# Moving a transform's last product behind another small product, its copies, and a dozen load times, in a fused FFT and mixture-of-experts kernel

## The chip, the cores and the metric

The kernel runs on one core of a Trainium2 chip. The metric is the device time of one execution, in microseconds (us), as the median of several runs. The core has a matrix engine (TensorE, PE in the profile; PEld is its weight load), a vector engine (VectorE, DVE), a scalar engine (ScalarE, ACT), a general engine (GpSimd, POOL) and a queue that issues nearly all transfers (SyncE, SP). Each runs its own instructions strictly in order.

## The reference

Everything is in 32-bit floats. A filter in the frequency domain runs along the sequence of each of 8 batches; its output, 24576 rows of 256, goes through a squared-ReLU layer and then through a soft mixture of experts whose slots are filled by a softmax over *all* rows:

```python
X = np.fft.rfft(x, axis=1)                       # x: 8 x 3072 x 256
y = np.fft.irfft(X * (filt_r + 1j * filt_i), n=3072, axis=1)
x = y.reshape(24576, 256)
h = np.maximum(x @ w_in, 0.0)                    # 256 -> 2048
x = h * h @ w_out                                # 2048 -> 256
logits = x @ phi                                 # 32 slots
d = softmax of logits over the rows;   slot_input = d.T @ x
slot_out[e] = np.maximum(slot_input[e] @ w1[e], 0.0) @ w2[e]   # 8 experts, 4 slots each
c = softmax of logits over the slots;  out = c @ slot_out
```

## The kernel before

The rows are cut into 48 chunks of 512, six per batch. A chunk is eight **pairs**; a pair makes two blocks of 128 of the hidden layer, each from six matmuls of 128x512 (lines 594 to 596: the data are split into a leading part `xo[:, 0]` and a remainder `xo[:, 1]`, the weights likewise). ACT takes each block out of PSUM with a ReLU (L601); the first block is squared on ACT (L603), the second on POOL (L605); DVE transposes both (L622). `xo` has two buffers, so a chunk's data are written while the chunk before runs.

The order of everything else is written out by hand. Time is counted in **units**: pair P stands at 2P, a chunk is 16 units, and within a pair there are four steps of half a unit, each with three of the six matmuls of a block. Work is put into five streams (`dsp`, `mv`, `late`, `fft`, `w`), each an event list with a unit as its due time; `run_streams` hands out what is due before and after each step, and holds back what needs PSUM banks until enough of the five side banks are free. "Unit 9.5 of a chunk" below is the due time modulo 16.

What is put there, and matters here:

- **Logits** (`logit`, L663): two groups of 16 matmuls in a chunk, at units 1.5 and 9.5, on a 128x32 division of the array.
- **Slots product** (`slot_in`, L793, `dispatch_events`): 32 matmuls on the same division, at unit 9.5 of the chunk that follows, right behind the logits. It reads `hd`, a rearranged copy of the hidden data that 16 transfers per chunk make (`move`, L651), and `eT`. For chunk 0 it is `slot_blocks` (L810), then `keep_block` and `sum_blocks`.
- **Inverse over n1** (`out_events`): the last product of the transform. `mm_y` (L514, 64 matmuls on a 64x64 division) reads `gin`, loaded by `load_g`; `even_y` (ACT) and two `unfold` (DVE, L531) undo a folding; `lead_y` (ACT, L539) writes the leading part of `xo` and `rest_y` (POOL, L546) its remainder, each once for either half `k` of the 256 columns. So 45 of the 48 chunks; three take another path.
- **Forward transform of the next batch** (`fft_events`): `load_x`, `fold_x` (an add on DVE, L155, and a subtraction on POOL, L156, for either `k`), `mm_a` (L165), stores to memory, then four rounds of `mm_b` (L299), filter `filt` (DVE, L310) and `join` (POOL, L319), and `mm_g2` (L218), with loads `load_f2` (filter, 1 MB), `load_s2`, `load_w` and `load_v`. Its wide tiles share three buffers.
- **The end**: the last chunk's softmax, the experts (`layer1`, `layer2`) and the output product. The experts' weights are loaded by `load_experts` into 6 tiles `w1t` (22 transfers of 256 KB), and into others.

Of the kernel before, what the change touches and what calls it, by code (L numbers as in the profile page):

```python
# [6 lines left out]
F32 = mybir.dt.float32  # L7
# [3 lines left out]
ALU = mybir.AluOpType  # L11
# [27 lines left out]
def body(tc, x, cA, cAf, fwp, fwd, ivp, inv, flt, cst, w_in, w_out, phi, w1, w2, out):  # L39
# [414 lines left out]
    def out_events(b, st, late):  # L454
# [92 lines left out]

        for g in range(NCB):
            if 6 * b + g not in (0, 1, 6):
                T = 96 * b + 16 * g - 12  # L550
                late(max(T - 14, 13.5), load_g, g)
                late(T, mm_y, g)
                late(T + 0.5, even_y, g)
                late(T + 1, unfold, g, ALU.add)
                late(T + 1.5, unfold, g, ALU.subtract)
                for k in range(2):
                    late(T + 5.5 + 2 * k, lead_y, g, k)
                    late(T + 6.5 + 2 * k, rest_y, g, k)
                continue
            T = 96 * b + 16 * g - 4  # L560
            put = late
            if T < 0:
                def put(t, fn, *a):
                    put0(ST["G0"] + ST["Gd"] * (t + 7), fn, *a)
            put(T - (5 if (b, g) == (0, 1) else 3), load_g, g)
            if T < 0:
                put(T - 1, warm)
            for k in range(2):
                put(T + k, mm_ai, g, k)
                put(T + k + 0.5, lead_ai, g, k)  # L570
                put(T + k + 0.5, rest_ai, g, k)
# [121 lines left out]


    run = {}

    def dispatch_events(c, put):
        q = 16 * (c + 1) + (2 if c else 6)
# [183 lines left out]
        if c == NCH - 1:  # L882
# [1 line left out]
                evac_l, gather, emax, expo, rescale, turn_e, turn_l, slot_blocks, keep_block, sum_block,  # L884
                row_max, row_exp, row_out, store_c,
            )
        put(q + .5, evac_l)
        put(q + 1.5, gather)
        put(q + 2.5, emax)
        put(q + 4, expo)  # L890
        put(q + 4, turn_l)
        put(q + 5, rescale)
        put(q + 5.5, turn_e)
        if c == 0:
            put(q + 7.5, slot_blocks)
            for r in range(4):
                put(q + 9 + .5 * r, keep_block, r)
            put(q + 11.5, sum_blocks)
        else:
            put(q + 7.5, slot_in)  # L900
            put(q + 9, accum)
# [199 lines left out]
    with tc.manual_schedule():  # L1101
        put, late = stream("fft"), stream("late")
# [14 lines left out]
        for j in range(4):  # L1117
# [3 lines left out]
            w = 1024 // len(ops)  # L1121
# [5 lines left out]
        for n in range(4):  # L1127
# [2 lines left out]
                wput(WO[n][1][k], conv_wo, n, k)  # L1130

        LEAD = [
            [[5.5] * 4, [3.5] * 4, [5] * 4, [5.5] * 4],
            [[5.5, 7.5, 15.25, 15.25], [6.5, 12.5, 13.5, 13.5], [5, 5.5, 10, 10], [5.5, 13, 15.25, 15.25]],
            [[20.25] + [15.25] * 3, [13.5] * 4, [20.5, 10, 10, 10], [8, 15.25, 15.25, 15.25]],
        ]

        opened = False
# [6 lines left out]
        for b in range(1, NB):  # L1145
            st = {}
            if b == 1:
                when = ([(22, 25, 28), (24, 29, 33.5), (27.5, 32, 36.5)], [47, 54.5, 65.5, 76.5], [53, 61.5, 70.5, 81.5])
            elif b == 2:
                when = ([(-19, -15.5, -10), (-11, -7, -3), (-5.5, -3, 0)], [13.5, 22, 38, 54], [18.5, 33.5, 49.5, 65.5])  # L1150
            else:
                when = ([(-35, -31, -26), (-23, -19, -14.5), (-22.5, -15.5, -10)], [1.5, 22, 38, 54], [17.5, 33.5, 49.5, 65.5])
            fft_events(b, lambda: G["fft"], stream("fft", 96 * (b - 1)), *when, dict(f=3, u=8, c=2, lead=LEAD[min(b, 3) - 1]), st)
            out_events(b, st, late)
        for c in range(NCH - 1):
            dispatch_events(c, stream("dsp"))
            if c:
                for n in range(4):
                    t = 0.5 * (n // 2)
                    for q, p in enumerate((14, 15, 16, 18) if c == 1 else (10, 11, 14, 18)):  # L1160
                        stream("mv", 16 * c)(p + t, move, c, q, n)
        for f in range(2, 8, 2):
            stream("mv", 16 * (NCH - 1))(5.5 + f / 2, late_turns, 2)
# [50 lines left out]
        w1t = []  # L1214
        for P in range(NP + 2):
            if P == 11:
                open_fft()
            if P == 48 * (NB - 1):
                G["fft_c"].__exit__(None, None, None)
                G["w1_c"], w1p = pool("w1p")  # L1220
                for n in range(6):
                    m = 4 if n < 5 else 2
                    w1t.append(w1p.tile([128, m * 512], F32, tag=f"w{n}", name="w1t"))
                    load_experts(w1t[-1], m, 0)
            if P == NP - 7:
                early = G["mlp"].tile([128, 8 * D], F32, tag="xo", name="wx", bufs=2)
                load_experts(early, 0, 3)
# [52 lines left out]
        w = (NB * N2 - 8) // 4  # L1280
# [6 lines left out]
        def load_call(n):  # L1287
            o = w * (n % 2)
            sync.dma_start(out=c_all[n // 2][:, o:o + w], in_=c_dr[:, 8 + w * n:8 + w * n + w])
# [6 lines left out]
        for r in range(4):  # L1296
            p = st["S"][r]
# [10 lines left out]
        load_experts(dsp.tile([128, 512], F32, tag="et", name="wx"), 0, 2)  # L1308
        load_experts(dsp.tile([128, 2 * 512], F32, tag="ac", name="wx"), 0, 3)
        row_max()  # L1310
        row_exp()
        row_out()
        store_c()
        load_call(3)
        p = bank("s0")
        for j in range(16):
            c4 = j % 4
# [6 lines left out]
        p = bank("s1")  # L1324
        for k in range(2):
            pe.matmul(p[:, 32 * k:32 * k + 32], af[:, 128 * k:128 * k + 128], s32, start=True, stop=True)
        si = dsp.tile([128, 2, NS], F32, name="si")
        vec.tensor_copy(si, p[:, 0:64].rearrange("p (k s) -> p k s", s=NS))
        vec.memset(zt, 0.0)

        hs.append([dsp.tile([128, 512], F32, tag="eT", name="hs", bufs=2) for h in range(2)])
# [51 lines left out]
        p = bank("s4")  # L1383
# [12 lines left out]
        for g in range(NG):  # L1396
            b, o = divmod(g, N2 // 4)
# [3 lines left out]
            for h in range(2):  # L1401
                p = bank(("s0", "s1", "s2", "s3")[ops % 4]).rearrange("p (a d) -> p a d", d=D)
# [166 lines left out]
```

## Time and profile before

| | |
|---|---|
| runs, us | 1882.72, 1887.92, 1883.05 (median 1883.05) |
| the profiled execution, us | 1880.15 |
| its span, us | 1878.2 |
| mean granted clock of TensorE | 0.994 |
| PE busy | 1824.0 us (97%) |
| DVE, ACT, POOL busy | 1206.0 (64%), 1034.8 (55%), 774.4 (41%) |
| matmuls of L594, L595, L596 | 626.6, 605.1 and 605.8 us |
| L663, L793, L514 (matmuls) | 186.3, 169.0, 53.2 us |

"Busy" is the share of the span in which an engine had an instruction running. Matmuls overlap: a 128x512 matmul is drawn 0.39 to 0.40 us long, while the next starts 0.23 us after it, so a gap of less than about 0.16 us between two doesn't show as idle time. The clock is the share of full speed that the chip granted TensorE: 1 is 2.4 GHz, and its other level is 1.2 GHz.

### The profile page before, as it was taken

Reading aid. Unit: us, or ns where it says so; the run is one execution under the profiler, and the core shown is the slowest. Engines: PE = TensorE matmul, PEld = TensorE weight load, DVE = VectorE, ACT = ScalarE, POOL = GpSimd, SP = SyncE. Lnnn points to the kernel's source line nnn. Section 1 sums busy time; section 2 is a strip of 40 time slices with the busy share of each in tenths; the row PEclk is TensorE's granted clock in tenths of the full one; section 3 lists DMA queues with packets and bytes.
Section 4 is the critical chain, followed back from the end, with each engine's and each line's share of the span. In section 5 each row is a group of like instructions: output and inputs, shape, how many; then the busy total and the mean of one; then the engine's idle time right before and its main releaser. Section 6 shows DMA issues by size and latency. Waiting matters only on the chain.

```text
span 1878.2 us, 42103 instructions
## 1 busy us (share of the span) xinstructions
PE 1824.0 (97%) x16326; PEld 1196.4 (64%) x16326; DVE 1206.0 (64%) x2267; ACT 1034.8 (55%) x1930; POOL 774.4 (41%) x812
## 2 busy tenths in 40 slices
PE   9999999999999999999999999999999999999987
PEld 6656566666666666666666666666666665666555
DVE  7946655766667666666567666666566755565558
ACT  6754455555555555555555555555555555455445
POOL 4043443534444544434444544444444533333224
PEclk9999999999999999999999999999999999999999
DMA  9768788886977697786978698787977677564989
GB/s 310 217 177 253 216 236 246 234 246 195 266 209 215 194 263 220 213 242 176 280 210 224 179 264 238 192 234 194 273 218 227 179 193 221 150 178 115 247 327 382
DMA packets 245813, 425.02 MB, mean 226 GB/s; under 512 B 25712, under 2 KB 103664, under 8 KB 245616
## 3 DMA queue, kind: packets, MB, share of 16 engines
q1 hardware_dynamic: 244744, 421.13, 77.6%
q8 instruction: 130, 2.13, 0.5%
q10 hardware_dynamic: 728, 1.15, 0.2%
q14 instruction: 67, 0.55, 0.1%
q0 software_dynamic: 144, 0.07, 0.0%
HBM read 151.71 MB, written 77.59 MB: 122 GB/s over the span
## 4 chain that ended last, share of the span: by engine, by line
PE 84%; DMA 6%; DVE 3%; SPq 3%; issue 2%; ACT 1%; POOL 0%; DVEq 0%; ACTq 0%
PE p L594 18%; PE p L596 17%; PE p L595 17%; PE sd L793 9%; PE L L663 8%; PE sd L299 3%; PE sd L514 2%; PE sd L218 2%; PE sd L165 2%; SPq L651 2%; DMA f<-x 2%; DMA hd<-hT 1%; DMA f<-flt 1%; DVE ct L1204 1%; PE pt L1193 1%
## 5 line engine op out<-in xcount | busy, mean ns | idle before, releaser
L601 ACT ACTIVATE h<-p 128x512 f32<-128x512 f32 x768 | 459.2, 598 | 545.8 <-PE p L596 527.9
L605 POOL TENSOR_TENSOR h<-h 128x512 f32<-128x512 f32 x375 | 393.7, 1050 | 816.6 <-ACT h L601 733.5
L622 DVE STREAM_TRANSPOSE hT<-h 128x512 f32<-128x512 f32 x736 | 490.2, 694 | 350.0 <-ACT h L603 295.4
L594 PE MATMUL p<-xo,wiH 128*128 128x512 f32 x1534 | 626.6, 408 | 0.0
L596 PE MATMUL p<-xo,wiL 128*128 128x512 f32 x1534 | 605.8, 395 | 0.0
L595 PE MATMUL p<-xo,wiH 128*128 128x512 f32 x1534 | 605.1, 394 | 0.0
L594 PEld LDWEIGHTS p<-xo,wiH 128*128 128x128 f32 x1534 | 288.5, 188 | 156.5 <-issue 81.8
L596 PEld LDWEIGHTS p<-xo,wiL 128*128 128x128 f32 x1534 | 288.7, 188 | 68.5
L595 PEld LDWEIGHTS p<-xo,wiH 128*128 128x128 f32 x1534 | 289.2, 188 | 58.7
L603 ACT ACTIVATE h<-h 128x512 f32<-128x512 f32 x393 | 249.0, 633 | 12.5
L319 POOL TENSOR_TENSOR u<-u 128x256 f32<-128x256 f32 x224 | 161.1, 742 | 131.1 <-DVE u L310 131.0
L663 PE MATMUL L<-h,wf 128*32 128x512 f32 x1536 | 186.3, 598 | 2.2 <-DVE wf L1017 1.8
L793 PE MATMUL sd<-hd,eT 128*32 128x512 f32 x1472 | 169.0, 597 | 6.9 <-DMA hd<-hT 6.9
L310 DVE TENSOR_TENSOR u<-sd,f 128x512 f32<-128x512 f32 x240 | 153.0, 676 | 16.4 <-DMA f<-flt 9.2
L793 PEld LDWEIGHTS sd<-hd,eT 128*32 128x32 f32 x1472 | 48.2, 111 | 119.3 <-issue 105.8
L546 POOL TENSOR_TENSOR xo<-gin,xo 128x512 fp32r<-128x512 f32 x90 | 119.1, 1324 | 0.0
L228 ACT ACTIVATE f<-sd 128x512 f32<-128x512 f32 x112 | 61.0, 608 | 87.3 <-PE sd L218 87.3
L854 DVE SCALAR_TENSOR_TENSOR ac<-ac,sc,sd 128x512 f32<-128x512 f32 x46 | 34.4, 748 | 105.9 <-PE sd L793 105.9
L663 PEld LDWEIGHTS L<-h,wf 128*32 128x32 f32 x1536 | 40.4, 109 | 95.2 <-issue 89.7
L712 DVE TENSOR_TENSOR lo<-L,lp 128x512 fp32r<-128x512 f32 x47 | 32.2, 685 | 73.3 <-ACT lp L711 73.2
L156 POOL TENSOR_TENSOR f<-f 128x512 f32<-128x512 f32 x42 | 54.1, 1288 | 57.0 <-DVE u L155 38.0
L769 DVE STREAM_TRANSPOSE eT<-et 32x128 f32<-32x128 f32 x184 | 72.3, 393 | 1.9
(161 smaller groups left out, 1596.8 us busy)
## 6 DMA issues: line engine op xcount, KB each, us to landing
hd<-hT SPq DMA_DIRECT2D x736, 256.0 KB
f<-flt SPq DMA_DIRECT2D x28, 1024.0 KB
gin<-G SPq DMA_DIRECT2D x47, 512.0 KB
out<-w1t SPq DMA_DIRECT2D x47, 512.0 KB
f<-x SPq DMA_DIRECT2D x84, 256.0 KB
S<-f SPq DMA_DIRECT2D x42, 512.0 KB
f<-S SPq DMA_DIRECT2D x112, 192.0 KB
G<-f SPq DMA_DIRECT2D x112, 192.0 KB
```

Source lines behind the costliest of these rows:

```text
L310: vec.tensor_tensor(out=u, in0=p.rearrange("p (h d) -> p h d", d=D), in1=f[:, 2 * r + k:2 * r + k + 1, :].to_broadcast([128, 2, D]), op=AL ...
L319: gps.tensor_tensor(out=a[:, h, :], in0=a[:, h, :], in1=b[:, 1 - h, :], op=ALU.add if h else ALU.subtract)
L546: gps.tensor_tensor(out=lo, in0=st["gi", g][:, k::2, :], in1=hi, op=ALU.subtract)
L594: pe.matmul(p, wh, x[:, 0, kk, :], start=(kk == 0), stop=False)
L595: pe.matmul(p, wh, x[:, 1, kk, :], start=False, stop=False)
L596: pe.matmul(p, wl, x[:, 0, kk, :], start=False, stop=(kk == 1))
L601: act.activation(out=h, in_=p, func=ACTF.Relu, scale=2.0 ** -8)
L603: act.activation(out=h, in_=h, func=ACTF.Square)
L605: gps.tensor_tensor(out=h, in0=h, in1=h, op=ALU.mult)
L622: vec.transpose(hT[c, f // 8][:, f // 4 % 2, :, o:o + 128], h2[P, k].rearrange("p (b t) -> p b t", b=4))
L663: pe.matmul(lg[c][32 * n:32 * n + 32, :], wf[:, f, :], h2.pop((P + n // 2, n % 2)), start=(f < 4), stop=(f >= FT - 4), tile_position=(0, 3 ...
L793: pe.matmul(S[32 * n:32 * n + 32, :], e[:, 32 * t:32 * t + 32], v, start=(t == 0), stop=(t == 3), tile_position=(0, 32 * n),)
```

## The change

Six things, all of them in the order; no arithmetic is added or removed.

1. `mm_y` moves from unit 4 to unit 9.5 of the chunk before its own, where it stands right behind `slot_in`. With it move `even_y` (4.5 to 10), both `unfold` (5 and 5.5 to 10.5), `lead_y` (9.5 and 11.5 to 11.5 and 13.5) and `rest_y` (10.5 and 12.5 to 12 and 14). `load_g` stays where it was.
2. Chunk 0's own steps (`evac_l` to `sum_blocks`) come 0.5 to 2 units earlier (list `FIRST`), and the transfers `move` of chunk 1 1.5 units earlier in three of four parts; the first fold and `mm_a` of batch 1 come 0.5 and 1.5 units earlier.
3. Batch 1's loads (`LEAD[0]`, in the order `load_w`, `load_v`, `load_f2`, `load_s2`, four rounds each) come up to 6.5 units earlier.
4. From batch 3 on, the first `load_x` comes 6 units earlier, and the first `load_s2` 2 units later.
5. The 22 transfers of `w1t` are spread over six places, unit 6 of chunks 42 to 46 and unit 12 of chunk 46, instead of all at once at the start of chunk 42.
6. At the end, the last chunk's `row_exp`, `row_out`, `store_c` and `load_call(3)` stand behind the product that gives `si` instead of ahead of it.

```diff
-                T = 96 * b + 16 * g - 12
-                late(max(T - 14, 13.5), load_g, g)
+                T = 96 * b + 16 * g - 6.5
+                late(max(T - 19.5, 13.5), load_g, g)
                 late(T, mm_y, g)
                 late(T + 0.5, even_y, g)
                 late(T + 1, unfold, g, ALU.add)
-                late(T + 1.5, unfold, g, ALU.subtract)
+                late(T + 1, unfold, g, ALU.subtract)
                 for k in range(2):
-                    late(T + 5.5 + 2 * k, lead_y, g, k)
-                    late(T + 6.5 + 2 * k, rest_y, g, k)
+                    late(T + 2 + 2 * k, lead_y, g, k)
+                    late(T + 2.5 + 2 * k, rest_y, g, k)
...
+    FIRST = [22, 23, 24, 25, 25, 26, 28]
...
         if c == 0:
-            put(q + 7.5, slot_blocks)
+            for t, fn in zip(FIRST, (evac_l, gather, emax, expo, turn_l, turn_e, slot_blocks)):
+                put(t, fn)
...
-            [[5.5] * 4, [3.5] * 4, [5] * 4, [5.5] * 4],
+            [[6.5, 6.5, 9.5, 9.5], [10, 7.5, 8, 10], [5, 6, 6.5, 6.5], [5.5, 10.5, 10, 10]],
...
-                when = ([(22, 25, 28), (24, 29, 33.5), (27.5, 32, 36.5)], ...
+                when = ([(22, 24.5, 26.5), (24, 29, 33.5), (27.5, 32, 36.5)], ...
...
-                when = ([(-35, -31, -26), (-23, -19, -14.5), (-22.5, -15.5, -10)], ...
+                when = ([(-41, -31, -26), (-23, -19, -14.5), (-22.5, -15.5, -10)], ...
...
-                    for q, p in enumerate((14, 15, 16, 18) if c == 1 else (10, 11, 14, 18)):
+                    for q, p in enumerate((12.5, 13.5, 14.5, 18) if c == 1 else (10, 11, 14, 18)):
...
-                for n in range(6):
-                    m = 4 if n < 5 else 2
-                    w1t.append(w1p.tile([128, m * 512], F32, tag=f"w{n}", name="w1t"))
-                    load_experts(w1t[-1], m, 0)
+            if P in (339, 347, 355, 363, 371, 374):
+                n = len(w1t)
+                m = 4 if n < 5 else 2
+                w1t.append(w1p.tile([128, m * 512], F32, tag=f"w{n}", name="w1t"))
+                load_experts(w1t[-1], m, 0)
...
         row_max()
-        row_exp()
-        row_out()
-        store_c()
-        load_call(3)
...
         vec.tensor_copy(si, p[:, 0:64].rearrange("p (k s) -> p k s", s=NS))
+        row_exp()
+        row_out()
+        store_c()
+        load_call(3)
```

On PE, in a chunk near the middle of the program, before: the inverse's group (L514) stands alone between two steps of three matmuls, behind the two matmuls of `gather` (L722, L723).

```order
L722 MATMUL sd<-lp,ss_t 128x512
L723 MATMUL sd<-lo,ss_t 128x512
L594 MATMUL p<-xo,wiH 128x512
L595 MATMUL p<-xo,wiH 128x512
L596 MATMUL p<-xo,wiL 128x512
L514 MATMUL sd<-cst_t,gin 64x2x32 x32
```

And now, in the same chunk, behind the logits (L663) and the slots product (L794 in the changed file, L793 before):

```order
L594 MATMUL p<-xo,wiH 128x512
L595 MATMUL p<-xo,wiH 128x512
L596 MATMUL p<-xo,wiL 128x512
L663 MATMUL L<-h,wf 32x512 x8
L794 MATMUL sd<-hd,eT 32x512 x16
L514 MATMUL sd<-cst_t,gin 64x2x32 x32
```

Three small products stand in one row where there were a row of two and one alone; this is so in 44 chunks (one x here is two matmuls of the trace).

On POOL, in the chunk of a batch in which the second third of the next batch is folded, before: `xo` is the remainder (`rest_y`), `f_...` a fold, `h` a square.

```order
L546 TENSOR_TENSOR xo<-gin,xo 128x512
L605 TENSOR_TENSOR h<-h 128x512
L546 TENSOR_TENSOR xo<-gin,xo 128x512
L156 TENSOR_TENSOR f_15373<-f_15373 128x512
L605 TENSOR_TENSOR h<-h 128x512
L156 TENSOR_TENSOR f_15373<-f_15373 128x512
```

And now:

```order
L605 TENSOR_TENSOR h<-h 128x512 x5
L546 TENSOR_TENSOR xo<-gin,xo 128x512
L156 TENSOR_TENSOR f_15336<-f_15336 128x512
L605 TENSOR_TENSOR h<-h 128x512
L546 TENSOR_TENSOR xo<-gin,xo 128x512
L156 TENSOR_TENSOR f_15336<-f_15336 128x512
```

The second remainder stood ahead of the fold; now a fold and one more square stand ahead of it. In the other chunks only the square does.

On SP, at the start of chunk 42, before: `hd` is a move, `w1t` the experts' weights.

```order
L460 DMA gin<-G 128x1024
L651 DMA hd<-hT 128x1x512 x12
L1085 DMA w1t<-w 128x512 x22
L651 DMA hd<-hT 128x1x512 x4
L880 DMA c_dr<-co 128x128
```

And now, from the same move on:

```order
L651 DMA hd<-hT 128x1x512 x16
L881 DMA c_dr<-co 128x128
L1089 DMA w1t<-w 128x512 x4
L460 DMA gin<-G 128x1024
L651 DMA hd<-hT 128x1x512 x16
```

The last four moves of a chunk no longer stand behind 22 weight transfers; four of these stand ahead of each of the next loads of `gin`.

## Rows read from the trace of the kernel before

**Rows 1.** Busy time by stretch: length, engines' busy us (count), clock, DMA share, GB/s.

```profile
110.00:305.00 195.00, 183.13 (x1688) 114.89 (x1684) 113.48 (x213) 97.83 (x184) 85.19 (x88) 0.98 0.80 222
305.00:1575.00 1270.00, 1265.44 (x11456) 826.29 (x11452) 819.92 (x1555) 708.24 (x1311) 566.77 (x583) 1.00 0.79 221
1595.00:1604.00 9.00, 5.29 (x27) 1.25 (x28) 1.31 (x3) 0.00 (x0) 0.00 (x0) 0.62 0.50 164
```

**Rows 2.** Timeline of PE: start, length, line, matmul, count; small products joined and alone.

```profile
1156.22 0.40 PE L596 MATMUL p<-xo,wiL 128*128 128x512 f32 x1
1156.55 1.92 PE L663 MATMUL L<-h,wf 128*32 128x512 f32 x16
1158.40 1.96 PE L299 MATMUL sd<-f,fw 48*32 48x256 f32 x64
...
1160.63 0.39 PE L595 MATMUL p<-xo,wiH 128*128 128x512 f32 x1
...
1197.96 1.16 PE L514 MATMUL sd<-cst_t,gin 64*64 64x64 f32 x64
...
1201.71 0.40 PE L596 MATMUL p<-xo,wiL 128*128 128x512 f32 x1
1202.04 1.96 PE L299 MATMUL sd<-f,fw 48*32 48x256 f32 x64
...
1204.26 0.39 PE L595 MATMUL p<-xo,wiH 128*128 128x512 f32 x1
...
1646.49 0.40 PE L596 MATMUL p<-xo,wiL 128*128 128x512 f32 x1
1646.82 1.92 PE L663 MATMUL L<-h,wf 128*32 128x512 f32 x16
...
1649.01 0.39 PE L595 MATMUL p<-xo,wiH 128*128 128x512 f32 x1
```

**Rows 3.** Timeline of PE: chunk 32's slots product and the first matmul of chunk 33.

```profile
1246.36 3.62 PE L793 MATMUL sd<-hd,eT 128*32 128x512 f32 x32
...
1258.40 0.40 PE L594 MATMUL p<-xo,wiH 128*128 128x512 f32 x1
```

**Rows 4.** Timeline of POOL in the same stretch: idle time and its releaser in brackets.

```profile
1253.95 1.04 POOL L605 TENSOR_TENSOR h<-h 128x512 f32<-128x512 f32 x1 [1.52 <-ACT h L601]
1254.95 1.35 POOL L546 TENSOR_TENSOR xo<-gin,xo 128x512 fp32r<-128x512 f32 x1
1256.48 1.04 POOL L605 TENSOR_TENSOR h<-h 128x512 f32<-128x512 f32 x1 [0.18 <-ACT h L601]
```

**Rows 5.** Timeline of POOL: the fold ahead of the start of chunk 35.

```profile
1328.81 1.30 POOL L156 TENSOR_TENSOR f<-f 128x512 f32<-128x512 f32 x1 [0.63 <-DVE u L155]
1330.07 1.49 POOL L605 TENSOR_TENSOR h<-h 128x512 f32<-128x512 f32 x1
```

**Rows 6.** Timeline of DVE, five places.

```profile
138.41 1.31 DVE L622 STREAM_TRANSPOSE hT<-h 128x512 f32<-128x512 f32 x2 [7.03 <-DMA hd<-hT]
...
223.07 1.29 DVE L310 TENSOR_TENSOR u<-sd,f 128x512 f32<-128x512 f32 x2 [6.64 <-DMA f<-flt]
...
875.00 0.69 DVE L155 TENSOR_TENSOR u<-f 128x512 f32<-128x512 f32 x1 [5.48 <-DMA f<-x]
...
1326.95 1.79 DVE L155 TENSOR_TENSOR u<-f 128x512 f32<-128x512 f32 x1
...
1787.32 0.48 DVE L1323 TENSOR_SCALAR af<-pt,fz 128x256 f32<-128x256 f32 x1
```

**Rows 7.** Timeline of SP: the issue of the experts' weights.

```profile
1575.53 15.46 SPq L1085 DMA_DIRECT2D w1t<-w  x22
```

**Rows 8.** Timeline of PE: a wait in chunk 5, and one in chunk 42.

```profile
262.94 3.48 PE L218 MATMUL sd<-u,iv 32*64 32x256 f32 x64 [3.07 <-DMA iv<-inv]
...
1590.79 1.03 PE L793 MATMUL sd<-hd,eT 128*32 128x512 f32 x6
1598.71 5.24 PE L793 MATMUL sd<-hd,eT 128*32 128x512 f32 x26 [6.88 <-DMA hd<-hT]
```

More of the change, by code (lines that the diff above doesn't have):

```diff
@@ L886, in dispatch_events @@
             )
[L887 to L893, printed above, removed]
-        if c == 0:
-            put(q + 7.5, slot_blocks)
+        if c == 0:
+            for t, fn in zip(FIRST, (evac_l, gather, emax, expo, turn_l, turn_e, slot_blocks)):
+                put(t, fn)
+        else:
+            put(q + .5, evac_l)
+            put(q + 1.5, gather)
+            put(q + 2.5, emax)
+            put(q + 4, expo)
+            put(q + 4, turn_l)
+            put(q + 5, rescale)
+            put(q + 5.5, turn_e)
+        if c == 0:
             for r in range(4):
-                put(q + 9 + .5 * r, keep_block, r)
-            put(q + 11.5, sum_blocks)
+                put(FIRST[-1] + 1 + .5 * r, keep_block, r)
+            put(FIRST[-1] + 3.5, sum_blocks)
         else:
@@ L1132, in body @@
         LEAD = [
-            [[5.5] * 4, [3.5] * 4, [5] * 4, [5.5] * 4],
+            [[6.5, 6.5, 9.5, 9.5], [10, 7.5, 8, 10], [5, 6, 6.5, 6.5], [5.5, 10.5, 10, 10]],
             [[5.5, 7.5, 15.25, 15.25], [6.5, 12.5, 13.5, 13.5], [5, 5.5, 10, 10], [5.5, 13, 15.25, 15.25]],
-            [[20.25] + [15.25] * 3, [13.5] * 4, [20.5, 10, 10, 10], [8, 15.25, 15.25, 15.25]],
+            [[20.25] + [15.25] * 3, [13.5] * 4, [20.5, 10, 10, 10], [6, 15.25, 15.25, 15.25]],
         ]
@@ L1147, in body @@
             if b == 1:
-                when = ([(22, 25, 28), (24, 29, 33.5), (27.5, 32, 36.5)], [47, 54.5, 65.5, 76.5], [53, 61.5, 70.5, 81.5])
+                when = ([(22, 24.5, 26.5), (24, 29, 33.5), (27.5, 32, 36.5)], [47, 54.5, 65.5, 76.5], [53, 61.5, 70.5, 81.5])
             elif b == 2:
@@ L1151, in body @@
             else:
-                when = ([(-35, -31, -26), (-23, -19, -14.5), (-22.5, -15.5, -10)], [1.5, 22, 38, 54], [17.5, 33.5, 49.5, 65.5])
+                when = ([(-41, -31, -26), (-23, -19, -14.5), (-22.5, -15.5, -10)], [1.5, 22, 38, 54], [17.5, 33.5, 49.5, 65.5])
             fft_events(b, lambda: G["fft"], stream("fft", 96 * (b - 1)), *when, dict(f=3, u=8, c=2, lead=LEAD[min(b, 3) - 1]), st)
```

## The prediction, made before the changed kernel ran

> **What bounds the kernel now.** The first view to read is busy time by stretch [rows 1]. From 305 to 1575 us, two thirds of the span, PE idles 1270 − 1265.44 = 4.6 us in all, at full clock, while DVE, ACT and POOL have a third to a little over a half of their time free. So the other engines and the transfers count only where PE waits for them; elsewhere the time is the number of matmuls and what lies between them. In the opening, 110 to 305, PE idles 195 − 183.13 = 11.9 us and the clock falls to 0.98 of full speed, which costs about another 195 × 0.02 = 3.9 (at the lower of the two levels everything takes twice as long). A third place is a hole of some 13 us near 1595. The reader should look for three things: what stands between matmuls, the few holes, and who will deliver PE's data last once work is moved.
>
> **The joined product.** PE's timeline [rows 2] gives the price of changing the way the array is divided. From the last full matmul (L596) ahead of a small product to the second full one (L595) behind it: the logits alone take 1649.01 − 1646.49 = 2.52 us, the L299 product alone 1204.26 − 1201.71 = 2.55, both in a row 1160.63 − 1156.22 = 4.41. Each span holds two full matmuls; 36 of them fill the stretch from the end of the slots product, 1246.36 + 3.62 = 1249.98, to the next chunk at 1258.40 [rows 3], so one takes 8.42 / 36 = 0.234 and two 0.47. Joining saves 2.52 + 2.55 − 0.47 − 4.41 = 0.19 us. The change does the same with L514, alone before [rows 2], in 44 chunks. Its 64x64 division behind a 128x32 one isn't in the trace; the nearest is this pair, also of two divisions. 44 × 0.19 = **8.4 us off**; from zero (the change of division inside the row costs as much as leaving it) to twice that.
>
> **Its copies.** This step can give it back. Before, the second remainder was written well ahead of the chunk's start. In chunk 32 take E = 1249.98, the end of the slots product, and S = 1258.40, the next chunk's first matmul [rows 3]; S = E + 8.4. POOL's last remainder ended at 1254.95 + 1.35 = 1256.30 [rows 4], 2.1 us before S. Now it is due 1.5 units later, behind the next square. That square began at 1256.48, with no copy ahead of its ReLU on ACT; the square before it, which had one (`lead_y` due at unit 11.5), began at 1253.95 [rows 4], and a pair is 12 × 0.234 = 2.8 us, so with a copy ahead it begins near 1256.75, ends near 1257.8, and the remainder ends near 1259.15, S + 0.75. PE needs it for its fifth matmul, at S + 4 × 0.234 = S + 0.94, whose weights are loaded one matmul ahead, at S + 0.7. So in an ordinary chunk it arrives just as it is wanted: 0 to 0.1 us late. 38 chunks: I take 0.5 us, bounds 0 and 4. The moved product itself hides nothing and needs nothing: E is 1.1 us later with S later by the same.
>
> In five chunks (11, 17, 23, 29, 35) a fold now stands ahead as well. Before chunk 35 the fold on POOL ran from 1328.81 to 1330.11, as DVE's add (1326.95, 1.79 long) let it go, and the square behind it from 1330.07 for 1.49 [rows 5, 6]. The remainder would follow at 1331.56 and end at 1332.9; that chunk's first matmul was at 1330.2 by the same 8.4 us, so it is wanted at 1330.9. That is 2.0 us late, 1.55 if the square takes 1.04 as in [rows 4]. I take 1.8: 5 × 1.8 = **9 us on**. Nothing hides it: PE has only that chunk's matmuls to do. It could be nothing, if POOL ran ahead, so the bounds are 0 and 12. In chunks 2 and 5 other work stands there; 1.5 us on for both.
>
> Why DVE's add took 1.79 us in one place and 0.69 in another [rows 6] bears on this: the long one began just as POOL ran a remainder. The Trainium skill's page "SBUF — State Buffer" (SBUF: two separate sides) says that a DVE operation with two SBUF inputs and a GpSimd operation exclude each other for a whole instruction. By that rule the next add of the fold could also get in ahead of the late remainder, and the nine would be about 12; the trace agrees with the rule where the two met.
>
> **The weights of the experts.** On SP, 22 transfers take 15.46 us to issue [rows 7] and stand between the moves of one chunk. The slots product that needs the last four stops after 6 of its matmuls, waits 6.88 us, and does the other 26 in 5.24 us instead of some 2.9, at a granted clock of 0.62 [rows 1, 8]: from 1590.79 to 1603.95 it takes 13.2 us where 3.62 is usual [rows 3]. Spread in fours, each group costs SP 4 × 15.46 / 22 = 2.8 us of issue, at unit 6, four units ahead of the moves. Behind them in SP's queue stands only a load of `gin` wanted some 19 units later. So the whole difference goes: **9.5 us off**, 7 if some moves are pushed.
>
> **The loads of x.** Once per batch from batch 3 on, DVE stood at the fold's first add until x arrived, 5.48 us in the worst case [rows 6], and everything behind it on DVE with it. There are five such places, and they make up nearly all of the 4.6 us idle in the long stretch; each also hides 0.16 us under the drawn length of a matmul (0.39 against 0.234), so 5.4 in all. The load comes 6 units earlier, ahead of the chunk's moves instead of between them; its buffer is free since `mm_b` one unit before. Late next are the moves behind it on SP, with most of a chunk in hand. **5 us off**, bounds 3 and 5.5.
>
> **The opening.** Idle and clock make 11.9 + 3.9 = 15.8 us, about 18 with what some 15 short waits hide. The causes are late transfers: DVE's transposes stood 7.03 us for the moves of chunk 1, the filter 6.64 us for its 1 MB load [rows 6], the product of round 4 3.07 us for `load_v` [rows 8], and the lower clock follows the two long ones. `load_v` and `load_s2` come 4 to 6.5 units earlier (a unit is 1.4 us of matmuls), each one unit behind the product that frees its buffer; that removes the third and most of the second. The moves of chunk 1 begin when `slot_blocks` has read its data, now three steps, 2.1 us, earlier: some 2 to 5 us of the first goes, with its clock. SP is full here, and what is moved ahead pushes something else; **12 us off**, bounds 5 and 17.
>
> **The end.** Four short DVE operations and a wait for ACT no longer stand ahead of `af` (1787.32, [rows 6]): 0.6 us at best, if the experts' last weights don't set the end anyway. I take 0.4 off.
>
> **The sum**, against the profiled execution's 1880.15: −8.4 + 0.5 + 9 + 1.5 − 9.5 − 5 − 12 − 0.4 = −24.3, so 1855.9. The runs shown lie 2.6 to 7.8 above that execution, their median 2.9; an execution of the changed kernel may be either, and I take **1857**.
>
> **The rivals.**
> *The folds don't delay the remainders* (POOL gets ahead because DVE's add finishes sooner with less else on DVE): the 9 is gone, 1848. For it: the add's 1.79 us is half waiting. Against: the remainder ran beside it before, and now does so again.
> *The opening keeps its holes*: SP's queue is in order and full, so earlier loads make the moves late; 8 us of the 12 stay and 1865. For it: idle time there has several causes in a row; against: each load is placed just behind what frees its buffer.
> *The joint saves nothing*, or the change doesn't do what it says on PE: 8.4 stays, 1865. Against it: two divisions in a row did save 0.19 here.
> *The remainder is late in every chunk* (the slower side). ACT now has the even half and both leading copies after the slots product, and POOL both remainders behind squares. If ACT falls one copy behind, the square and the remainder behind it are late by up to a square's 1.04 us in the 38 ordinary chunks: 38 × 1.04 = 39.5 on, 1857 + 39.5 = 1896.5. It decides from a delay of 26 / 38 = 0.68 us in each. For it: the reserve that I worked out is nil. Against: POOL idled 1.52 and 0.18 us ahead of those two squares [rows 4], so a small delay of its own is caught up.
>
> **How the numbers follow.** The forecast gets 0.55 with 1849 to 1866, folds without delay 0.13, the opening 0.16, the joint 0.06, all remainders late 0.10 (half of it short of the deciding point). The range 1845 to 1872 leaves out the far side of the first and most of the last. About 0.3% (5.6 us) is what a measurement of this kernel can tell from no change: slower needs nearly the whole of the last rival, 0.05; within 0.3%, 1877.4 to 1888.7, takes half of that delay or two other failures together, 0.06; faster 0.89.
>
> **What would show it.** Right: PE's row at unit 9.5 as logits, slots product, L514 without gaps, and no L514 alone; in chunks 11, 17, 23, 29 and 35 a wait of L595 for POOL's remainder of 1.5 to 2 us just after the first matmuls, and none over 0.1 in the others; the slots product of chunk 42 at 3.6 us, clock 1.00; no DVE wait for x over 1 us after 305; idle time of 110 to 305 below 5 us. Wrong: waits for POOL or ACT at the start of every chunk, new waits for moves (`hd`) at the slots product, or idle time on PE from 305 to 1575 above 15 us.

## The result and the profile after

The changed kernel takes 1860.44 us (median of 4 runs, 1857.41 to 1863.38); the kernel before, on the same chip, 1882.88 (4 runs, 1877.41 to 1887.92). The ratio is 0.9881, 95% interval 0.9864 to 0.9898. The profiled execution took 1859.09 us, its span is 1857.3 and its mean clock 0.996. The forecast was 1857. The total is near it, but by two misses that cancel: in the opening the kernel gained some 7 us more than the sum had, and a loss of nearly 9 us was not in the sum at all.

Where the 20.9 us between the two spans went, by the starts of chunks in PE's timeline (chunk 0 by its first layer matmul, the others by their first L594):

| stretch | before, us | after, us | difference |
|---|---|---|---|
| start to chunk 0 | 54.98 | 58.82 | +3.8 |
| chunk 0 to chunk 7 | 280.46 | 261.72 | -18.7 |
| chunk 7 to the end of the last L596 | 1434.91 | 1429.93 | -5.0 |
| from there to the end | 107.80 | 106.81 | -1.0 |

The first row has the same instructions in both kernels. All twelve other profiles of this study, that of before among them, reach chunk 0 at 54.6 to 56.3 us: 58.82 is a trait of this one execution.

Busy time by stretch, of after, columns as in [rows 1]:

```profile
110.00:305.00 195.00, 193.61 (x1841) 122.07 (x1844) 128.44 (x239) 110.12 (x206) 91.77 (x94) 1.00 0.87 248
305.00:1575.00 1270.00, 1258.67 (x11427) 824.15 (x11420) 820.58 (x1546) 703.52 (x1303) 567.17 (x581) 1.00 0.79 220
1570.00:1640.00 70.00, 70.00 (x485) 48.08 (x484) 43.13 (x88) 40.48 (x75) 24.78 (x23) 1.00 0.69 195
```

The opening is nearly full: PE idles 1.4 us where [rows 1] had 11.9, at full clock. The hole near 1595 is gone: the stretch around chunk 42 has no idle time. But the long stretch idles more than before, 1270 - 1258.67 = 11.3 us against 4.6. What PE waits for in it (line and tile that wait, what they wait for, us in total, times, longest):

```profile
PE p L595 <- POOL xo L546: 7.2, 5, 1.4
PE sd L299 <- DMA f<-S: 4.1, 9, 1.0
```

The first line was forecast, the second was not. DVE's waits for x, which were to go, are gone from this stretch.

**The joined product.** PE's timeline in chunk 32:

```profile
1232.14 0.39 PE L596 MATMUL p<-xo,wiL 128*128 128x512 f32 x1
1232.46 1.93 PE L663 MATMUL L<-h,wf 128*32 128x512 f32 x16
1234.20 3.62 PE L794 MATMUL sd<-hd,eT 128*32 128x512 f32 x32
1237.75 1.16 PE L514 MATMUL sd<-cst_t,gin 64*64 64x64 f32 x64
...
1239.18 0.39 PE L595 MATMUL p<-xo,wiH 128*128 128x512 f32 x1
...
1247.34 0.40 PE L594 MATMUL p<-xo,wiH 128*128 128x512 f32 x1
...
1282.77 0.40 PE L594 MATMUL p<-xo,wiH 128*128 128x512 f32 x1
```

From L596 to L595 the row takes 1239.18 - 1232.14 = 7.04 us. The last two rows are the starts of chunks 33 and 34: 35.43 us apart. Before, chunk 33 began at 1258.40 [rows 3] and chunk 34 at

```profile
1294.02 0.40 PE L594 MATMUL p<-xo,wiH 128*128 128x512 f32 x1
```

which makes 35.62. So 0.19 us per chunk, as forecast; in the last seven chunks of the inverse (40 to 46) it is 0.12 to 0.17.

**The copies.** POOL ahead of chunk 33, an ordinary one, which starts at 1247.34:

```profile
1245.68 1.04 POOL L605 TENSOR_TENSOR h<-h 128x512 f32<-128x512 f32 x1 [0.45 <-ACT h L601]
1246.68 1.29 POOL L546 TENSOR_TENSOR xo<-gin,xo 128x512 fp32r<-128x512 f32 x1
```

The second remainder ends at 1247.97, 0.63 us behind the start, where [rows 4] had it 2.1 ahead, and PE doesn't wait. Ahead of chunk 35, which starts at 1318.21, a fold comes between:

```profile
1314.75 1.35 POOL L546 TENSOR_TENSOR xo<-gin,xo 128x512 fp32r<-128x512 f32 x1
1316.73 1.30 POOL L156 TENSOR_TENSOR f<-f 128x512 f32<-128x512 f32 x1 [0.63 <-DMA hd<-hT]
1317.99 1.49 POOL L605 TENSOR_TENSOR h<-h 128x512 f32<-128x512 f32 x1
1319.44 1.26 POOL L546 TENSOR_TENSOR xo<-gin,xo 128x512 fp32r<-128x512 f32 x1
```

The remainder ends at 1320.70, and PE, which has used up what needs only the first half, stands for it:

```profile
1318.91 0.40 PE L594 MATMUL p<-xo,wiH 128*128 128x512 f32 x1
1320.75 0.50 PE L595 MATMUL p<-xo,wiH 128*128 128x512 f32 x1 [1.44 <-POOL xo L546]
```

1320.75 - 1318.91 - 0.23 = 1.61 us, and the same to 0.01 in the other four such chunks: 8.05 us.

**The new wait.** SP and PE around the start of chunk 12 (499.58):

```profile
490.13 8.22 SPq L651 DMA_DIRECT2D hd<-hT  x8
498.39 3.37 SPq L206 DMA_DIRECT2D f<-S  x4
```

```profile
502.48 1.92 PE L663 MATMUL L<-h,wf 128*32 128x512 f32 x16
504.33 1.49 PE L299 MATMUL sd<-f,fw 48*32 48x256 f32 x34
506.54 1.09 PE L299 MATMUL sd<-f,fw 48*32 48x256 f32 x30 [0.72 <-DMA f<-S]
```

`f<-S` is the first `load_s2` of a batch, whose tile the first `mm_b` (L299) reads. It is issued behind eight moves, 1.2 us ahead of the chunk that wants it. Before, its issue stood 11.8 us ahead of that chunk (502.48, with the chunk at 514.32). The step from chunk 12 to 13 takes 34.67 us where 33.33 is what it takes without the wait (experiment 2). In chunks 12, 18, 24, 30 and 36 the loss is 1.34, 2.13, 1.26, 2.28 and 1.80: 8.8 us.

**The weights.** Chunk 42 has no gap, and SP issues four weight loads well ahead of the moves:

```profile
1570.61 2.04 SPq L1089 DMA_DIRECT2D w1t<-w  x4
...
1583.54 16.96 SPq L651 DMA_DIRECT2D hd<-hT  x16
```

```profile
1579.86 3.62 PE L794 MATMUL sd<-hd,eT 128*32 128x512 f32 x32
1583.41 1.16 PE L514 MATMUL sd<-cst_t,gin 64*64 64x64 f32 x64
```

The chunk takes 31.45 us, as its neighbours do, and took 41.11. These rows also show that the moves begin where the slots product ends (1579.86 + 3.62 = 1583.48): it has then read `hd`.

### The profile page after: what moved, and what is told of

The parts are those of the page before. It is cut to its first block, busy times and chain, and to the rows that moved or that the text cites. A ratio compares the mean times of both kernels' runs of the same rounds, so it can differ in the third digit from the quotient of the medians.

```text
span 1857.3 us, 42036 instructions
## 1 busy us (share of the span) xinstructions
PE 1812.1 (98%) x16326; PEld 1192.9 (64%) x16326; DVE 1212.9 (65%) x2267; ACT 1033.4 (56%) x1930; POOL 776.3 (42%) x812
## 3 DMA queue, kind: packets, MB, share of 16 engines
q8 instruction: 130, 2.13, 0.5%
## 4 chain that ended last, share of the span: by engine, by line
PE 84%; DMA 5%; DVE 3%; SPq 2%; issue 2%; ACT 1%; POOL 1%; POOLq 0%; DVEq 0%; ACTq 0%
PE p L594 18%; PE p L595 17%; PE p L596 17%; PE L L663 9%; PE sd L794 8%; PE sd L218 3%; PE sd L299 3%; PE sd L514 2%; PE sd L165 2%; DMA f<-S 2%; SPq L651 1%; DMA hd<-hT 1%; DVE ct L1208 1%; PE pt L1197 1%; PE pt L1410 1%
## 5 line engine op out<-in xcount | busy, mean ns | idle before, releaser
L622 DVE STREAM_TRANSPOSE hT<-h 128x512 f32<-128x512 f32 x736 | 485.3, 692 | 250.4 <-ACT h L603 230.4
L594 PE MATMUL p<-xo,wiH 128*128 128x512 f32 x1534 | 621.7, 405 | 0.1
L595 PE MATMUL p<-xo,wiH 128*128 128x512 f32 x1534 | 605.6, 395 | 7.2 <-POOL xo L546 7.2
L596 PE MATMUL p<-xo,wiL 128*128 128x512 f32 x1534 | 605.8, 395 | 0.0
L594 PEld LDWEIGHTS p<-xo,wiH 128*128 128x128 f32 x1534 | 288.1, 188 | 122.4 <-issue 43.9
L595 PEld LDWEIGHTS p<-xo,wiH 128*128 128x128 f32 x1534 | 288.6, 188 | 70.0 <-POOL xo L546 9.4
L596 PEld LDWEIGHTS p<-xo,wiL 128*128 128x128 f32 x1534 | 288.3, 188 | 68.4
L603 ACT ACTIVATE h<-h 128x512 f32<-128x512 f32 x393 | 248.4, 632 | 12.5
L663 PE MATMUL L<-h,wf 128*32 128x512 f32 x1536 | 186.9, 599 | 2.2 <-DVE wf L1021 1.8
L531 DVE TENSOR_TENSOR gin<-gin,sd 128x512 f32<-128x512 f32 x90 | 61.8, 687 | 182.7 <-ACT gin L522 181.2
L522 ACT ACTIVATE gin<-sd 128x512 f32<-128x512 f32 x45 | 26.9, 598 | 256.7 <-PE sd L514 256.7
L794 PE MATMUL sd<-hd,eT 128*32 128x512 f32 x1472 | 166.3, 592 | 0.0
L310 DVE TENSOR_TENSOR u<-sd,f 128x512 f32<-128x512 f32 x240 | 152.7, 675 | 11.5 <-PE sd L299 10.1
L794 PEld LDWEIGHTS sd<-hd,eT 128*32 128x32 f32 x1472 | 47.8, 110 | 110.1 <-issue 106.8
L663 PEld LDWEIGHTS L<-h,wf 128*32 128x32 f32 x1536 | 40.0, 109 | 96.2 <-issue 91.4
```

Source lines behind the costliest of these rows:

```text
L310: vec.tensor_tensor(out=u, in0=p.rearrange("p (h d) -> p h d", d=D), in1=f[:, 2 * r + k:2 * r + k + 1, :].to_broadcast([128, 2, D]), op=AL ...
L594: pe.matmul(p, wh, x[:, 0, kk, :], start=(kk == 0), stop=False)
L595: pe.matmul(p, wh, x[:, 1, kk, :], start=False, stop=False)
L596: pe.matmul(p, wl, x[:, 0, kk, :], start=False, stop=(kk == 1))
L603: act.activation(out=h, in_=h, func=ACTF.Square)
L622: vec.transpose(hT[c, f // 8][:, f // 4 % 2, :, o:o + 128], h2[P, k].rearrange("p (b t) -> p b t", b=4))
```

## The experiments

Each is the changed kernel, or the kernel before where said, with the edit shown. Times are medians; the ratio is to the kernel before on the same chip.

| run | us | ratio, 95% interval |
|---|---|---|
| after | 1860.4 | 0.9881 (0.9864 to 0.9898) |
| 1: after without the joint | 1870.0 | 0.9921 (0.9906 to 0.9935) |
| 2: after, `load_s2` at its old time | 1849.1 | 0.9813 (0.9797 to 0.9829) |
| 3: before with the joint alone | 1876.5 | 0.9960 (0.9945 to 0.9975) |
| 4: as 2, folds one unit later | 1848.2 | 0.9810 (0.9794 to 0.9827) |
| 5: after with the old opening | 1873.1 | 0.9951 (0.9933 to 0.9968) |
| 6: after, batch 1's loads at their old times | 1871.0 | 0.9936 (0.9913 to 0.9958) |
| 7: after, `w1t` at once | 1866.8 | 0.9913 (0.9891 to 0.9934) |
| 8: after, load of x at its old time | 1861.5 | 0.9885 (0.9861 to 0.9910) |
| 9: as 2, folds apart | 1842.4 | 0.9784 (0.9762 to 0.9807) |
| 10: after, first steps at their old times | 1866.3 | 0.9897 (0.9868 to 0.9927) |
| 11: before with the load of x alone | 1879.3 | 0.9982 (0.9970 to 0.9994) |

**1. Without the joint.** The inverse's product and its copies go back to their old places; everything else stays.

```diff
-                T = 96 * b + 16 * g - 6.5
-                late(max(T - 19.5, 13.5), load_g, g)
+                T = 96 * b + 16 * g - 12
+                late(max(T - 14, 13.5), load_g, g)
...
-                    late(T + 2 + 2 * k, lead_y, g, k)
-                    late(T + 2.5 + 2 * k, rest_y, g, k)
+                    late(T + 5.5 + 2 * k, lead_y, g, k)
+                    late(T + 6.5 + 2 * k, rest_y, g, k)
```

> The changed kernel with the inverse over n1 back at its old place and its copies at their old units; everything else stays changed. My theory, that the joint saves 0.2 us in each of 44 chunks and that its copies cost 1.6 us in five of them: L514 stands alone again at 1.29 us over its neighbours, the five waits of L595 for POOL's remainder are gone, and the two nearly cancel: the changed kernel's time + 8.9 - 8 = 1 us more, within 3. The waits for the load of S at the start of five chunks stay as they are, about 8.8 us together. Rival, that the copies also slow the ordinary chunks: the time falls by 3 us or more. Rival, that the waits for the load of S come from the moved copies (ACT or SP held up by them): those five waits are gone too, and the time falls by some 8.

It took 1870.0, so the joint is worth some 10 us here and not about nothing. The two terms of the sum are both there: ordinary chunks take 35.65 again, and the five waits for POOL are gone. But the waits for `load_s2` grew, from 8.8 to 3.17 + 3.67 + 2.58 + 2.79 + 2.25 = 14.5 us. SP ahead of chunk 12, which starts at 503.66 here:

```profile
495.32 8.21 SPq L651 DMA_DIRECT2D hd<-hT  x8
503.58 3.23 SPq L206 DMA_DIRECT2D f<-S  x4
```

The moves start 503.66 - 495.32 = 8.3 us ahead of the next chunk, and 499.58 - 490.13 = 9.45 with the joint. The moves start at the end of the slots product; the inverse's product, 1.1 us of PE, used to stand ahead of it and now stands behind. So every transfer behind the moves gains 1.1 us against PE: five places, 5.7 us. My sum had said that the moved product "hides nothing and needs nothing".

The rest of the 10 us lies in the opening. Chunk 0 to chunk 7 takes 269.99 us here, 8.3 more than in the changed kernel. Of these, 1.9 are in chunk 0, which takes 35.95 us here and in experiments 2 and 6, but 34.1 to 34.4 in the ten other profiles, whatever the edit. From chunk 1 to chunk 7 it is

| chunk 1 to chunk 7, us | old opening | new opening |
|---|---|---|
| without the joint | 246.1 (before), 249.1 (11) | 234.0 (this run) |
| with the joint | 248.4 (3), 244.9 (5) | 227.6 to 229.3 (after, 2, 4, 7, 8, 9) |

With the old opening the joint brings nothing that these profiles can tell; with the new one it brings 4.8 to 6.4 us, of which four joined products at 0.19 make 0.8. PE idles 195 - 190.75 = 4.3 us from 110 to 305 here, and 1.4 with the joint:

```profile
110.00:305.00 195.00, 190.75 (x1805) 119.08 (x1804) 121.21 (x224) 106.09 (x198) 87.78 (x92) 1.00 0.85 241
```

```profile
PE sd L724 <- DVE lo L713: 1.4, 2, 0.8
PE sd L218 <- DVE gin L531: 1.4, 2, 0.8
```

These are the longest of its waits there, the one for `gather`'s data and the other put down to `unfold`, which the joint moves away. Whether that or the earlier moves make the difference, no run tells.

**2. `load_s2` back.** One number: unit 8 instead of 6, ahead of the moves.

```diff
-            ... [20.5, 10, 10, 10], [6, 15.25, 15.25, 15.25]],
+            ... [20.5, 10, 10, 10], [8, 15.25, 15.25, 15.25]],
```

> The changed kernel with the first load of S back at 8 units ahead of its product, from batch 3 on, as before; nothing else is changed. My theory: at 6 units it stands on SP behind eight moves, at 8 ahead of them; so the waits of 1.3 to 2.3 us at the first product of rounds in chunks 12, 18, 24, 30 and 36 vanish, 8.8 us together: 1860.4 - 8.8 = 1851.6, and SP issues this load some 10 us earlier against its chunk's start. Rival, that the load waits for the stores of S to land, wherever it stands: the waits stay and the time is the changed kernel's.

1849.1, which is 11 us off the changed kernel by the medians; the five waits are gone and chunks 12, 18, 24, 30 and 36 take 33.33 each, 8.8 us less together, as the theory had it. SP ahead of chunk 12, which starts at 498.27:

```profile
484.27 1.79 SPq L206 DMA_DIRECT2D f<-S  x4
488.82 12.92 SPq L651 DMA_DIRECT2D hd<-hT  x12
```

The load stands ahead of the moves and is issued 14.0 us before the chunk, not 1.2. This settles the cause of the second wait: edit 4 itself, through SP's order.

**3. The joint alone**, on the kernel before (the reverse of the diff of experiment 1).

> The kernel before with the first part of the change alone: the inverse over n1 behind the slots product, and its copies. My theory: 44 x 0.2 = 8.9 us off, 5 x 1.6 = 8 us on for the remainders behind a fold, so -1 us against the kernel before, between -4 and +3: no difference that can be seen. All its old holes stay: 110 to 305 us idle some 12 us, the wait in chunk 42 some 9.5. Rival, that the joint brings more where the holes are (PE's small products no longer stand where the loads are late): 5 us or more off. Rival, that the late remainders fall in more chunks when the loads are late too: 5 us or more on.

1876.5, that is some 8 us faster than before, where the sum of my terms for the joint and its copies was about zero. Joint and fold waits are as in the changed kernel (chunks of 35.43, five of 37.10). But the five gaps at the loads of x are gone too, with the load at its old place: chunk 22 takes 35.65, and took 38.25. In the kernel before, the only waits that the profile lists for PE from 305 to 1575 us were these five, of `gather` for DVE's `lo`, which stands behind the late add:

```profile
PE sd L723 <- DVE lo L712: 4.6, 5, 2.3
```

Here no such wait is left. DVE still waits for x there,

```profile
876.12 0.69 DVE L155 TENSOR_TENSOR u<-f 128x512 f32<-128x512 f32 x1 [4.03 <-DMA f<-x]
```

but the add now starts 6.6 us into the chunk (869.56), and 8.0 before [rows 6: 875.00, chunk at 866.98]. Of those 1.5 us the moves' earlier start gives 1.1 (858.61 before, 8.4 ahead of the chunk; 860.10 here, 9.5 ahead), and `lo` is in time. So the gain that I had given to the load of x can be had from the joint.

**4. Folds one unit later**, on top of 2: behind the second remainder, both in a row.

```diff
-                when = ([(-41, -31, -26), (-23, -19, -14.5), (-22.5, -15.5, -10)], ...
+                when = ([(-41, -31, -26), (-23, -18, -14.5), (-22.5, -15.5, -10)], ...
```

> The changed kernel with the first load of S back at 8 units, and the two folds of the second third of x, from batch 3 on, one unit later (units 14 and 15 instead of 13 and 14), so that on POOL the second remainder stands ahead of them. My theory: the five waits for S and the five for the remainder all vanish: 1860.4 - 8.8 - 8 = 1843.6, with the product of that third, due 2.5 units after its last fold, not late. Rival, that the fold then comes late for its own product (1 to 2 us at each of five places): 1850. Rival, that the remainder is late for other reasons: the five waits of L595 stay, 1851.6.

1848.2, no more than 1 us off. POOL around the start of chunk 35:

```profile
1306.11 1.74 POOL L546 TENSOR_TENSOR xo<-gin,xo 128x512 fp32r<-128x512 f32 x1
1307.82 2.98 POOL L156 TENSOR_TENSOR f<-f 128x512 f32<-128x512 f32 x2
1310.77 1.04 POOL L605 TENSOR_TENSOR h<-h 128x512 f32<-128x512 f32 x1
```

The remainder is in time but for 0.2 us. Now the first square of the chunk stands behind two folds, and the logits, which read it, wait (weight loads of PE):

```profile
1311.85 0.14 PEld L663 LDWEIGHTS L<-h,wf 128*32 128x32 f32 x2 [0.88 <-POOL h L605]
```

In each of the five places 1.61 us became 0.20 + 1.01; by their lengths the five chunks gain 0.39 each, 2 us. The wait moved to another reader of POOL's work.

**9. Folds apart**, also on top of 2: remainder, fold, square, fold, square.

```diff
-                put(TF + k, fold_x, s, k)
+                put(TF + (2 if b > 2 and s == 1 else 1) * k, fold_x, s, k)
...
-                when = ([(-41, -31, -26), (-23, -19, -14.5), (-22.5, -15.5, -10)], ...
+                when = ([(-41, -31, -26), (-23, -18, -14.5), (-22.5, -14, -10)], ...
```

> The changed kernel with the first load_s2 back at its old time, and from batch 3 on the second third folded one unit later, its two folds two units apart instead of one, the last third 1.5 units later: POOL then has remainder, fold, square, fold, square. Theory (each of the five places lost 1.61 us because a fold stood ahead of the second remainder, and 1.2 us when both folds stood together ahead of the next square, which the logits wait for): nothing is left there, 5 x 1.6 = 8 us off the kernel with the load alone, 1849 - 8 = 1841. Rival (POOL simply has too much work between the slots product and the next logits, whatever the order): the wait goes on to the product mm_a or the logits, 1847 to 1849.

1842.4 (1840.8 to 1844.7): the theory's 1841 is within the spread, and no wait of over 0.2 us is left in the five places. Those 0.2 us of the remainder stay, so the five chunks take 35.73 instead of 37.10: 6.9 us and not 8. POOL around the start of chunk 35:

```profile
1302.52 1.74 POOL L546 TENSOR_TENSOR xo<-gin,xo 128x512 fp32r<-128x512 f32 x1
1304.22 1.29 POOL L156 TENSOR_TENSOR f<-f 128x512 f32<-128x512 f32 x1
1305.47 1.03 POOL L605 TENSOR_TENSOR h<-h 128x512 f32<-128x512 f32 x1
1307.34 1.28 POOL L156 TENSOR_TENSOR f<-f 128x512 f32<-128x512 f32 x1 [0.83 <-DVE u L155]
1308.58 1.49 POOL L605 TENSOR_TENSOR h<-h 128x512 f32<-128x512 f32 x1
```

POOL even idles 0.83 us there, so it was the order of its work and not the amount that made PE wait. In the long stretch PE now idles 0.2 us of 1270:

```profile
305.00:1575.00 1270.00, 1269.82 (x11566) 834.46 (x11559) 822.24 (x1565) 712.79 (x1321) 575.32 (x586) 1.00 0.79 222
```

This version beats both kernels: 2.2% off the kernel before, 18 us off the changed one.

**5. The old opening**: all of edit 2 and edit 3 undone.

```diff
-            [[6.5, 6.5, 9.5, 9.5], [10, 7.5, 8, 10], [5, 6, 6.5, 6.5], [5.5, 10.5, 10, 10]],
+            [[5.5] * 4, [3.5] * 4, [5] * 4, [5.5] * 4],
...
-    FIRST = [22, 23, 24, 25, 25, 26, 28]
+    FIRST = [22.5, 23.5, 24.5, 26, 26, 27.5, 29.5]
...
-                    for q, p in enumerate((12.5, 13.5, 14.5, 18) if c == 1 else (10, 11, 14, 18)):
+                    for q, p in enumerate((14, 15, 16, 18) if c == 1 else (10, 11, 14, 18)):
```

(The steps behind `slot_blocks` and the first fold and its product go back too.)

> The changed kernel with its whole opening as before: the steps of chunk 0, the moves of chunk 1, the first fold and product of batch 1, and batch 1's load times. Theory (the opening was worth some 18 us: idle time of PE between 110 and 305 fell from 11.9 to 1.4 us, the clock rose from 0.98 to 1.00, short waits went): 1860 + 18 = 1878, the idle time of that stretch back at 10 us or more, with DVE's wait for the moves of chunk 1 and its wait for the filter. Rival 1, the term of my sum: 1860 + 12 = 1872. Rival 2 (the joint alone would have closed part of these holes, as it closed the gaps at the loads of x): 1866 or less.

1873.1: 13 us by the medians (0.0070 of 1883), where an interval of some 5 us either way holds both my term and the theory. The profile is sharper: chunk 0 to chunk 7 takes 279.3 us, and 261.7 in the changed kernel, 17.6 more. The opening idles 10.9 us again, at a clock of 0.97,

```profile
110.00:305.00 195.00, 184.12 (x1752) 116.61 (x1752) 113.63 (x215) 98.78 (x185) 83.98 (x87) 0.97 0.79 224
```

and the two long waits of DVE in [rows 6] are back:

```profile
138.64 1.31 DVE L622 STREAM_TRANSPOSE hT<-h 128x512 f32<-128x512 f32 x2 [6.96 <-DMA hd<-hT]
...
220.35 1.29 DVE L310 TENSOR_TENSOR u<-sd,f 128x512 f32<-128x512 f32 x2 [6.88 <-DMA f<-flt]
```

**6. Batch 1's loads alone at their old times**: the first hunk of 5.

> The changed kernel with batch 1's load times alone as before; the steps of chunk 0, the moves of chunk 1 and the first fold stay early. Theory (the loads' lateness carries most of the opening: the filter's 6.64 us with the clock that fell behind it, and the 3.07 us for load_v): 1860 + 11 = 1871, DVE waiting for the filter and PE for iv. Rival (the moves of chunk 1 carry it, and the loads find room once these go early): 1860 + 4 = 1864.

1871.0, as the theory had it. What DVE and PE wait for in the opening:

```profile
DVE u L310 <- DMA f<-flt: 7.4, 2, 6.2
...
PE sd L218 <- DMA iv<-inv: 4.7, 2, 3.3
```

**10. The first steps alone at their old times**: 5 without its first hunk.

> The changed kernel with the steps of chunk 0, the moves of chunk 1 and batch 1's first fold and product at their old times, its loads at their new ones. Theory (the two halves of the opening add up: all of it cost 12.7 us, the loads alone 10.5): 1860 + 2 = 1862. Rival (the earlier loads need the early steps of chunk 0, or stand ahead of what these want): 1867 or more, with DVE waiting for the moves of chunk 1 as before.

1866.3 (1860.5 to 1867.9), nearer to the rival. DVE stands 6.45 us ahead of its transposes again, though the profile puts the end of this wait down to ACT's ReLU and not to the moves, and PE waits behind it:

```profile
139.83 0.47 PE L723 MATMUL sd<-lp,ss_t 128*128 128x512 f32 x1 [2.76 <-DVE ac L860]
```

From chunk 0 to chunk 7 the three profiles take 12.2 us (10), 16.3 (6) and 17.6 (5) more than the changed kernel. The two halves don't add up: each undone alone brings back most of the loss. The loads and the steps of chunk 0 are needed together. The medians of 6 and 10 are too uncertain to tell that.

**7. The weights at once.**

```diff
-            if P in (339, 347, 355, 363, 371, 374):
-                n = len(w1t)
+                for n in range(6):
```

> The changed kernel with the 22 transfers of w1t issued at once at the start of chunk 42. Theory: the hole at that chunk's slots product returns at its old price, 1860 + 9.5 = 1870, 9 to 10 us in that one place. Rival (with the inverse's product behind the slots product the wait is longer or shorter, since gin and the moves stand elsewhere): below 1866 or above 1874.

1866.8, by the medians 6 us (an interval of some 5 either way); the place itself is clear. PE in chunk 42:

```profile
1580.23 1.03 PE L794 MATMUL sd<-hd,eT 128*32 128x512 f32 x6
1587.44 5.83 PE L794 MATMUL sd<-hd,eT 128*32 128x512 f32 x26 [6.18 <-DMA hd<-hT]
1593.20 1.16 PE L514 MATMUL sd<-cst_t,gin 64*64 64x64 f32 x64
```

It is the hole of [rows 8], and chunk 42 takes 40.87 us instead of 31.45: 9.4.

**8. The load of x at its old time**, and **11. the load of x alone**, the reverse of this diff on the kernel before.

```diff
-                when = ([(-41, -31, -26), ...
+                when = ([(-35, -31, -26), ...
```

> The changed kernel with the first load of x from batch 3 on at its old time. My sum gave this edit 5 us: 1860 + 5 = 1865, with five gaps of up to 2.5 us on PE near the first fold. Rival, from the joint alone, in which those five gaps were gone with the load at its old place: 1860, no gap there, DVE's wait for x of some 5 us still in the records but with nothing late behind it; the waits of L299 for load_s2 stay at 8.8 us, or fall, if the earlier load of x was what delayed them.

> The kernel before with one edit: the first load of x from batch 3 on 6 units earlier. The five gaps of before (0.66, 0.78, 2.63, 1.29 and 0.59 us more than in a chunk beside) are removed by the joint alone, as two runs showed. If the two edits are two cures of one gap, this one alone removes them as well: 5 to 5.5 us off the kernel before, 1883 - 5.4 = 1878, chunks 10, 16, 22, 28 and 34 at 35.6 us each. If the earlier load does nothing (its buffer comes free late, or the moves pushed behind it are as late), 1883 and the gaps stay.

Run 8 took 1861.5, 1 us from the changed kernel, with chunks 10, 16, 22, 28 and 34 at 35.44 as there; the waits for `load_s2` came to 11.2 us in it. Run 11, on the kernel before, took 1879.3, and those five chunks take 35.63 each where they took 36.20 to 38.25; by the chunks' lengths 5.9 us, by the medians 3 to 5. So each of the two edits closes the five gaps alone, and the second to come finds nothing to do. In the changed kernel the load of x is worth nothing that these runs can tell.

## Why the prediction was right in total, and where it was not

Term by term, forecast and measured in the traces:

- **The joint**, -8.4: the rows gave 0.19 per chunk, and 0.19 it is, for the new pair of divisions too; 33 chunks at 0.16 to 0.19 and 7 at 0.12 or more, and the few in the opening, make some 8.
- **Ordinary copies**, +0.5: nothing. The remainder ends 0.63 us behind the chunk's start; the step that put it at 0.75 held. The rival with all remainders late didn't come.
- **Folds**, +9: 8.05. Place, number, waiting line and length were as forecast (1.61 each for 1.55 to 2.0). The bound of 12 needed a DVE add ahead of the late remainder. The Trainium skill's page "SBUF — State Buffer" (SBUF: two separate sides) says that a DVE operation with two SBUF inputs and a GpSimd operation that reads SBUF exclude each other. The trace agrees: ahead of chunk 35 the add that met the first remainder took 1.79 us, the next, which got in first, took 0.78 and the square beside it 1.49 instead of 1.04. But that add came ahead of the square, not of the remainder, and its 0.45 us was in the row that I had used already.
- **The weights**, -9.5: 9.5 against before and 9.4 in experiment 7; the same hole costs 8.6 and 8.5 in experiments 3 and 11.
- **The loads of x**, -5: the gaps are gone, but this was counted for the wrong edit. The joint closes them by itself (3, 8); the sum holds only because the two cures overlap and I had given the joint no such effect. The step that failed is "the moved product itself hides nothing and needs nothing": that had E, the end of the slots product, and S, the next chunk's start, move together, but E comes 1.1 us earlier against S (1247.34 - 1237.82 = 9.5 us where [rows 3] give 8.4), and with E the moves.
- **The opening**, -12 with +1.5 for chunks 2 and 5: chunk 0 to chunk 7 fell by 18.7, but these edits alone don't do it. Without the joint they bring 246.1 - 234.0 = 12.1 us from chunk 1 to chunk 7 (experiment 1), so the forecast 12 was right for them, and its discount ("SP is full here, and what is moved ahead pushes something else") isn't shown to be wrong. The other 4.8 to 6.4 us come from the joint, which brings them only with the new opening. The step that failed is again "hides nothing and needs nothing"; by what path it failed here stays open. The 1.5 for chunks 2 and 5 can't be told apart within these sums. Nor would the same price have held edit by edit: experiments 6 and 10 show that the loads and the first steps need each other.
- **The end**, -0.4: not to be told. The tail was 107.8 before and 106.8 after, but from 106.0 to 108.9 over the other profiles, with the old order as with the new.
- **The missing term**: `load_s2` 2 units later, +8.8. My text listed it in edit 4 and costed only the load of x beside it. SP's order shows the price: an issue 11.8 us ahead of its chunk became one 1.2 us ahead, behind eight moves of 1.0 us each. The prediction's own question, "who will deliver PE's data last once work is moved", put to this load would have found it.

The last three rows of the table of stretches add up to -24.7, against the -24.3 forecast, and +3.8 of this execution's start leaves the 20.9 between the spans. So the total was right by luck, as misses cancelled: the opening some 7 us better than its two terms (17.9 without the 0.8 of joined products, against 12 - 1.5), the new wait 8.8 worse, all the rest some 2 better.

## What to carry to other kernels

Cost every moved load by the queue it is issued from: how long before its reader it is issued, what stands ahead of it there, before and after. When a product moves on the engine that bounds the kernel, ask also what its old place was holding back: here 1.1 us of PE ahead of the slots product delayed 16 transfers in every such chunk, and all that stood behind them. Where one in-order engine serves two readers, a late copy is cured by spreading the work ahead of it between their due times; moving it in one block only moves the wait.

## What the runs showed of the hardware

The price of one late transfer is not fixed. With the same order on SP around these loads, the five waits for `load_s2` came to 8.8, 8.0, 8.2, 10.8, 11.2 and 8.3 us in the profiles of the changed kernel and of experiments 5, 6, 7, 8 and 10, and a single one of them to anything from 0.4 to 5.5 us (chunk lengths less 33.33). That may be part of why medians that differ by 3 us couldn't be told apart here. A load with reserve removes it: experiments 2, 3, 4 and 9 have 33.33 in all five.

Twelve of the thirteen profiles, with equal instructions there, reach chunk 0 at 54.6 to 56.3 us, and one at 58.8; 4 us of a profile can thus come from the first 60 us alone, and two profiles are better compared from a landmark behind it.
